# Two groups of heads, one pair of banks: where the third batch's first outputs are put

## Chip, core and metric

The kernel runs on one core of one Trainium2 chip. The metric is the device time of one execution in microseconds; lower is better. All sums of matrix products are kept in PSUM, a memory of 128 partitions with eight banks of 2 KB each; a bank holds 512 float32 per partition. TensorE (PE) writes it, VectorE (DVE) and ScalarE (ACT) read it.

## What is computed

Retention, a linear attention with a decay per head, followed by a bilinear feed-forward layer without biases:

```
q, k, v: (8 batches, 8 heads, 576 positions, 64)        float32
gamma[h] = 1 - 2**(-5-h)
scores   = (q @ k^T) / sqrt(64)
ret      = scores * gamma[h]**(i-j)   where i >= j, else 0
attn     = ret @ v
x        = attn as (8*576 = 4608 tokens, 8*64 = 512)
out      = ((x @ w_a) * (x @ w_b)) @ w_out               w_a, w_b: 512 x 1536, w_out: 1536 x 512
```

## The kernel before

**Stages.** The 4608 tokens pass through the feed-forward layer in blocks (`blocks`: 512, 256, 256, then seven of 512). `ffn_block` computes, for each of 12 slices of 128 hidden columns, a product with `w_a` (`pa`, line L794) and one with `w_b` (`pb`, L809). ACT copies the first out of PSUM (L802), and DVE multiplies it by the second (L814). Then come the products with `w_out` (`po`, L828), which ACT or DVE copy out for the store (L837, L839). Matrix operands are bfloat16, sums float32.

**Retention runs in between.** The input `x` of a block is made ahead of it by the retention of the same tokens. The first 256 positions of batches 0, 1 and 2 are done in six steps (`STEPS`): a step is one batch and one half of its heads, four heads. Steps 4 and 5 are the two halves of batch 2, and these six steps hold only the first 256 positions. Their results are the input of the second feed-forward block (tokens 512 to 767). The rest of retention runs later in larger pieces (`stretch`).

**The pieces of one step.** The positions of a step are split into an early half (`a` = 0) and a late one (`a` = 1), 128 each.

- `score_step` multiplies keys by queries within the halves (L347) into a tile `sc` of two banks. DVE masks it into `sT` (L355).
- `state_products` and `state_copies` sum keys times values into a state per half (`kv`, L374). ACT copies the first half's state to `state_after` (L386), and both states to `own` and `second` (L390, L391).
- `step_states` (L421) multiplies the late half's queries by the state after the early half: two matmuls of 128 columns that write the bank of `a` = 1.
- `step_keys` (L437) multiplies values by masked scores: 16 small matmuls (64 x 64, 128 columns), eight into each bank, added to what `step_states` left in the bank of `a` = 1.
- `close_step` (L448) scales the outputs with `qs_o` on DVE and writes them to the tile `x` of the block.

**Where outputs stand.** An output tile is `[128, 2, 512]` float32, so two whole banks, one for each `a`. A step uses the first 256 columns of each. There are eight banks: four for the pool `ps_ffn` (one each), two for `ps_sc` (one tile) and two for `ps_o` (one tile). In the third batch, `score_step(4)` takes `ps_sc` and `score_step(5, ps_o[0], "o")` takes `ps_o`. The outputs of step 4 are then opened in `ps_sc`, and those of step 5 in `ps_o`, each in the banks of its own scores. The next writer of `ps_o` is `keyed` of the first `stretch` (L538), and the next of `ps_sc` is `matched` in the same stretch (L600).

**Accumulation.** A matmul with `start=True` marks its whole bank, on the partitions it writes, as not yet written. A later one without `start` overwrites where the mark stands and adds elsewhere.

**Order.** The order of each engine's instructions is the order in which the program issues them (`manual_schedule`). `ffn_block` yields after each matmul, and a list `todo` holds the functions with the amount of work at which they are due: `third_turn` at 124, `third_states` at 128, `third_outputs` at 136, all in the output projection of the first block. The framework sets the waits between engines from the tiles that instructions read and write. Each engine works through its queue in order, so an instruction that waits holds up all behind it on its engine.

Of the kernel before, what the change touches and what calls it, by code (L numbers as in the profile page):

```python
# [18 lines left out]
def kernel(  # L19
# [108 lines left out]
    def half(i):  # L128
        return slice(64 * i, 64 * i + 64)
# [205 lines left out]
    def queries(key, r, j, a):  # L335
        return transposed[key][r, 0].rearrange(
            "p (k j s) -> p j k s", k=2, j=2)[:, j, :, half(a)]
# [71 lines left out]
    outputs = {}  # L409

    def open_step(i, place=None):
        if place is None:
            outputs[i] = ps_o[0].tile([128, 2, 512], FP32, tag="o", name="o0")
        else:
            outputs[i] = place.tile([128, 2, 512], FP32, tag="sc", name="o0")

    def step_states(i, first):

        n, hh = STEPS[i]
        for j in (0, 1):  # L420
            nc.tensor.matmul(outputs[i][:, 1, 128 * j:128 * j + 128],  # L421
                             state_after[:, n % 2, 2 * hh + j, :],
                             queries((n, hh), slice(0, 128), j, 1),
                             start=(first and j == 0), stop=True,
                             skip_group_check=True)

    def step_keys(i, fresh):

        n, hh = STEPS[i]
        vb = natural[n, hh][1]  # L430
        sT = scored.pop((n, hh))
        seen = set()
        for j in (0, 1):
            for kp in (0, 1):
                for a, r in QUADS:
                    e0 = kp * 256 + (2 * j + r) * 64
                    nc.tensor.matmul(  # L437
                        outputs[i][half(r), a, 128 * j:128 * j + 128],
                        vb[half(a), e0:e0 + 64],
                        sT[half(a), r, j, kp],  # L440
                        start=(a in fresh and (a, r) not in seen), stop=True,
                        skip_group_check=True)
                    seen.add((a, r))

    def close_step(i):
        n, hh = STEPS[i]
        cs = slice(2 * hh, 2 * hh + 2)
        nc.vector.tensor_tensor(  # L448
            x_of(256 * n, 256)[:, cs]
            .rearrange("p j (a s) -> p a j s", a=2),  # L450
            outputs.pop(i)[:, :, 0:256]
            .rearrange("p a (j s) -> p a j s", j=2),
            qs_o[:, cs]
            .rearrange("p j (a s) -> p a j s", a=2), op=ALU.mult)
# [517 lines left out]

    def third_outputs():
        open_step(4, ps_sc)
        open_step(5)
        for i in (4, 5):
            step_states(i, True)
        for i in (4, 5):
            step_keys(i, {0})
            close_step(i)  # L980

    def third_turn():
        for i in (4, 5):
# [3 lines left out]
            (112.1, cast_step, (5, Q, "act")),  # L987
            (124, third_turn, ()), (128, third_states, ()),
            (136, third_outputs, ())]
    todo += [(60 + 10 * n, total_of, (n,)) for n in (0, 1)]  # L990
    todo += [(136, total_of, (2,))]
# [74 lines left out]
```

## Time and profile before

| | |
|---|---|
| three runs | 325.1, 326.3, 326.32 us (median 326.3) |
| profiled execution | 325.12 us |
| its span, first to last instruction | 323.4 us |
| PE busy | 317.7 us (98%) |
| DVE, ACT, POOL busy | 165.8 (51%), 131.5 (41%), 118.2 us (37%) |
| products `pa`, `pb`, `po` busy on PE | 108.8, 111.5, 97.0 us |
| scaling of a step (L448) | 0.680 to 0.692 us each, six of them |
| key products of a step (L437) | 16, 0.42 us from the first's start to the last's end |
| granted clock of TensorE | 1.00 |

Times count from the start of the span. In a line of the timeline the first number is the start, the second the duration from the first of a run of like instructions to the end of the last, then engine, line, operation, tiles written and read, shapes and count; what stands in brackets is the engine's idle time before it and what ended that. Matmuls overlap on PE: the next one starts before the last one's end. In a line of the groups, the numbers behind the bar are busy time, the mean duration in ns, and the idle time just before.

### The profile page before, as it was taken

What the parts mean: (1) busy time and instruction counts of PE and PEld (TensorE: products, weight loads), DVE (VectorE), ACT (ScalarE), POOL (GpSimd) and SP (SyncE); (2) the same over time, 40 slices, a digit from 0 to 9 for tenths busy, and PEclk for the clock granted to TensorE, in tenths of its full rate; (3) what the DMA queues carried; (4) which work ended last, traced back from release to release, by engine and by line L of the source; (5) the groups of instructions that cost most, each with busy time, mean ns of one, the idle gap of its engine ahead of it and who ended that gap; (6) DMA issues with size and microseconds to landing.
All of it is one profiled execution on the core that took longest, in us unless ns stands there. A gap on an engine that the chain in (4) does not pass through costs nothing.

```text
span 323.4 us, 8669 instructions
## 1 busy us (share of the span) xinstructions
PE 317.7 (98%) x3611; PEld 164.5 (51%) x3611; DVE 165.8 (51%) x294; ACT 131.5 (41%) x293; POOL 118.2 (37%) x158
## 2 busy tenths in 40 slices
PE   7899999999999999999999999999999999999996
PEld 3564457778444555454454545454445444444444
DVE  5734445665546754835374627561666256514311
ACT  7744853463435533533253324442433243313321
POOL 4990067574655375357075206450520000000000
PEclk9999999999999999999999999999999999999999
DMA  8999999999999999999899169935740520031013
GB/s 215 256 199 205 253 233 203 199 176 206 175 233 234 217 199 244 221 227 226 180 216 191 60 155 197 205 76 146 170 108 23 108 68 2 2 97 32 1 24 108
DMA packets 145431, 50.90 MB, mean 157 GB/s; under 512 B 126704, under 2 KB 140912, under 8 KB 145392
## 3 DMA queue, kind: packets, MB, share of 16 engines
q1 hardware_dynamic: 140112, 45.37, 68.6%
q0 software_dynamic: 4752, 4.72, 8.9%
q8 instruction: 28, 0.46, 0.6%
q10 hardware_dynamic: 528, 0.26, 0.3%
q14 instruction: 11, 0.09, 0.1%
HBM read 37.75 MB, written 9.44 MB: 146 GB/s over the span
## 4 chain that ended last, share of the span: by engine, by line
PE 94%; DMA 2%; SPq 2%; ACT 1%; DVE 1%; issue 0%; DVEq 0%
PE pb L809 29%; PE po L828 29%; PE pa L794 28%; DMA qf<-in_q_dram 2%; SPq L159 2%; PE sc L600 1%; PE o L628 1%; PE o L641 1%; PE kv L538 1%; PE pa L771 1%; ACT state_after L386 0%; PE o L437 0%; PE kv L374 0%; PE sc L347 0%; PE tp L329 0%; DVE hT L814 0%
## 5 line engine op out<-in xcount | busy, mean ns | idle before, releaser
L814 DVE TENSOR_TENSOR hT<-ha,pb 128x512 bf16<-128x512 bf16 (+1 forms) x120 | 75.9, 634 | 94.2 <-PE pb L809 86.0
L802 ACT CAST ha<-pa 128x512 bf16<-128x512 f32 (+1 forms) x120 | 64.8, 543 | 115.5 <-PE pa L794 111.2
L809 PE MATMUL pb<-xT,wb_sb 128*128 128x512 bf16 (+1 forms) x480 | 111.5, 358 | 0.1
L794 PE MATMUL pa<-xT,wa_sb 128*128 128x512 bf16 (+1 forms) x468 | 108.8, 357 | 0.0
L828 PE MATMUL po<-wo_sb,hT 128*128 128x512 bf16 (+2 forms) x456 | 97.0, 368 | 0.0
L809 PEld LDWEIGHTS <-wb_sb 128*128 128x128 bf16 x480 | 47.0, 98 | 46.5 <-issue 0.3
L794 PEld LDWEIGHTS <-wa_sb 128*128 128x128 bf16 x468 | 45.1, 98 | 44.4 <-issue 0.2
L828 PEld LDWEIGHTS <-hT 128*128 128x128 bf16 x456 | 42.8, 98 | 47.1
L484 POOL CAST qkb<-qf 64x1024 bf16<-64x1024 f32 x15 | 15.4, 1030 | 67.4 <-DMA qf<-in_q_dram 61.0
L495 POOL TENSOR_TENSOR vb<-vf,vs 128x1024 bf16<-128x1024 f32 (+1 forms) x17 | 28.8, 1699 | 13.2 <-DMA vf<-in_v_dram 8.2
L839 DVE COPY osb<-po 128x512 f32<-128x512 f32 (+2 forms) x17 | 11.1, 653 | 43.2 <-PE po L828 43.2
L837 ACT COPY osb<-po 128x512 f32<-128x512 f32 (+1 forms) x21 | 12.0, 573 | 43.3 <-PE po L828 43.3
L484 POOL CAST qkb<-kf 64x1024 bf16<-64x1024 f32 (+1 forms) x17 | 15.9, 933 | 14.5 <-DMA kf<-in_k_dram 13.9
L563 DVE TENSOR_TENSOR sums<-kv,sums 128x256 f32<-128x256 f32 x44 | 18.6, 424 | 2.8 <-PE kv L538 0.8
L609 DVE TENSOR_TENSOR sT<-sc,mask 128x512 bf16<-128x512 f32 x30 | 19.5, 681 | 0.0
L488 POOL CAST qkb<-kf 64x512 bf16<-64x512 f32 (+1 forms) x34 | 18.8, 580 | 1.0
L488 POOL CAST qkb<-qf 64x512 bf16<-64x512 f32 x30 | 17.6, 614 | 0.6
L567 ACT CAST states<-sums 64x512 bf16<-64x512 f32 x26 | 16.0, 617 | 0.3
L654 DVE TENSOR_TENSOR xT<-o,qs 128x512 bf16<-128x512 f32 x24 | 15.4, 682 | 1.5 <-PE o L641 1.5
L311 POOL CAST qkb<-kf 128x512 bf16<-128x512 f32 x5 | 3.1, 614 | 16.7 <-DMA kf<-in_k_dram 16.7
L855 PE MATMUL w<-ones 128*128 128x512 bf16 x19 | 6.8, 476 | 1.5 <-DVE idxp_f L204 1.5
L355 DVE TENSOR_TENSOR sT<-sc,mask_s 128x1024 bf16<-128x1024 f32 x6 | 7.2, 1222 | 1.3 <-PE sc L347 1.2
(88 smaller groups left out, 163.9 us busy)
## 6 DMA issues: line engine op xcount, KB each, us to landing
qf<-in_q_dram SPq DMA_DIRECT2D x32, 256.0 KB, 4.8
vf<-in_v_dram SPq DMA_DIRECT2D x32, 256.0 KB, 5.1
kf<-in_k_dram SPq DMA_DIRECT2D x31, 256.0 KB, 5.0
out_dram<-osb SPq DMA_DIRECT2D x25, 256.0 KB, 2.4
out_dram<-osb SPq DMA_DIRECT2D x21, 128.0 KB, 3.0
wo_sb<-in_moe_w_out_dram POOLq DMA_DIRECT2D x3, 512.0 KB, 16.7
qf<-in_q_dram SPq DMA_DIRECT2D x8, 128.0 KB, 3.2
kf<-in_k_dram SPq DMA_DIRECT2D x8, 128.0 KB, 3.4
```

Source lines behind the costliest of these rows:

```text
L484: nc.gpsimd.tensor_copy(qkb[0:64, w, e], t[0:64, e])
L488: nc.gpsimd.tensor_copy(to[:, :, 1 - r], fro[:, :, r])
L495: nc.gpsimd.tensor_tensor(vb[:, e].rearrange("p (h d) -> p h d", d=D), t[:, e].rearrange("p (h d) -> p h d", d=D), decay[:, at], op=ALU.mult)
L563: nc.vector.tensor_tensor(sums[:, i], own, prev, op=ALU.add)
L567: nc.scalar.copy(to(half(1 - r)), fro(half(r)))
L609: nc.vector.tensor_tensor(sT[:, on].rearrange("p c k s -> p (c k) s"), sc[:, on].rearrange("p c k s -> p (c k) s"), mask3.unsqueeze(1).to_ ...
L654: nc.vector.tensor_tensor(x_of(t0, 128).rearrange("p c (a s) -> p c a s", a=2), o[:, :, :, kp].rearrange("p a c s -> p c a s"), qs[:, :, s ...
L794: nc.tensor.matmul(pa[:, 0:n], wa_sb[:, c, fs], xT[:, c], start=(c == 0), stop=(c == NC - 1))
L802: nc.scalar.copy(ha[:, 0:n], pa[:, 0:n])
L809: nc.tensor.matmul(pb[:, 0:n], wb_sb[:, c, fs], xT[:, c], start=(c == 0), stop=(c == NC - 1))
L814: nc.vector.tensor_tensor(hT[:, F, 0:n], has[F][:, 0:n], pb[:, 0:n], op=ALU.mult)
L828: nc.tensor.matmul(po[:, 0:width], hT[:, F, u * 128:(u + 1) * 128], wo_sb[:, F, cols], start=(F == 0), stop=(F == NF - 1))
```

## The change

Only `third_outputs` is changed:

```diff
     def third_outputs():
         open_step(4, ps_sc)
-        open_step(5)
+        outputs[4], outputs[5] = (outputs[4][:, :, half] for half in
+                                  (slice(0, 256), slice(256, 512)))
         for i in (4, 5):
-            step_states(i, True)
+            step_states(i, i == 4)
         for i in (4, 5):
-            step_keys(i, {0})
+            step_keys(i, {0} if i == 4 else set())
             close_step(i)
```

The outputs of step 5 no longer have a tile of their own in `ps_o`. They use columns 256 to 511 of the two banks in `ps_sc` whose columns 0 to 255 hold the outputs of step 4. Since `start` marks a whole bank, only step 4's matmuls set it; step 5's first ones find the mark and overwrite. The order of the program stays: state products of 4 and 5, key products of 4, scaling of 4, key products of 5, scaling of 5.

## Prediction

> **What bounds the kernel now.** I read the page's first and fourth parts, then the timeline of each engine around the two output products of the third batch, then the waits of PE behind them.
>
> ```profile
> PE 317.7 (98%) x3611; PEld 164.5 (51%) x3611; DVE 165.8 (51%) x294; ACT 131.5 (41%) x293; POOL 118.2 (37%) x158
> ...
> PE 94%; DMA 2%; SPq 2%; ACT 1%; DVE 1%; issue 0%; DVEq 0%
> ```
>
> PE is busy for 98% of the span and makes up 94% of the chain that ended last. So anything that makes PE stand still in the middle of the kernel is paid at the end, unless PE would have stood still later anyway. The groups of PE instructions from 48.7 us to the end answer that. Their last column is the idle time ahead of them:
>
> ```profile
> L794 PE MATMUL pa<-xT,wa_sb 128*128 128x512 bf16 (+1 forms) x432 | 100.7, 355 | 0.0
> L809 PE MATMUL pb<-xT,wb_sb 128*128 128x512 bf16 (+1 forms) x432 | 100.6, 355 | 0.1
> L828 PE MATMUL po<-wo_sb,hT 128*128 128x512 bf16 (+2 forms) x416 | 87.9, 367 | 0.0
> ```
>
> Every PE group there has 0.0 or 0.1 us of idle. There is no later wait in which a delay of PE could be lost. The place itself, on PE (start, duration, instruction, count):
>
> ```profile
> 45.28 0.29 PE L374 MATMUL kv<-vb,qkb 64*64 64x64 bf16 x16
> 45.41 0.42 PE L347 MATMUL sc<-qkT 64*64 64x128 bf16 x16
> 45.66 0.29 PE L374 MATMUL kv<-vb,qkb 64*64 64x64 bf16 x16
> 45.89 1.90 PE L828 MATMUL po<-wo_sb,hT 128*128 128x512 bf16 x8
> ...
> 47.63 0.28 PE L421 MATMUL o<-qkT,state_after 128*128 128x128 bf16 x2
> ...
> 47.91 0.27 PE L421 MATMUL o<-qkT,state_after 128*128 128x128 bf16 x2
> 48.11 0.42 PE L437 MATMUL o<-sT,vb 64*64 64x128 bf16 x16
> ...
> 48.36 0.39 PE L437 MATMUL o<-sT,vb 64*64 64x128 bf16 x16
> 48.69 1.90 PE L828 MATMUL po<-wo_sb,hT 128*128 128x512 bf16 x8
> 50.42 0.60 PE L794 MATMUL pa<-xT,wa_sb 128*128 128x256 bf16 x4
> ```
>
> The L421 pairs at 47.63 and 47.91 are the state products of steps 4 and 5. The sixteens of L437 at 48.11 and 48.36 are their key products. DVE and ACT at the same place:
>
> ```profile
> 45.50 2.36 DVE L355 TENSOR_TENSOR sT<-sc,mask_s 128x1024 bf16<-128x1024 f32 x2
> 48.58 1.29 DVE L448 TENSOR_TENSOR xT<-o,qs_o 128x512 bf16<-128x512 f32 x2 [0.72 <-PE o L437]
> ...
> 46.04 1.09 ACT L386 CAST state_after<-kv 64x128 bf16<-64x128 f32 x4 [1.13 <-PE kv L374]
> ```
>
> Today both key products run back to back on PE, and the two scalings (L448) follow on DVE while PE is already in the output projection (L828). The first scaling starts at 48.58, in the middle of step 5's key products, and holds PE up in nothing, because it reads the banks of step 4 while PE writes those of step 5.
>
> **The change, part by part.**
>
> 1. *A wait goes.* Step 5's state products used to land in the banks that held step 5's scores, so they waited for the second masking (L355) to read them out. It ends at 45.50 + 2.36 = 47.86, and the second L421 pair starts at 47.91. Two such products last 0.28 us together at 0.22 us each, so their starts lie 0.056 us apart, and without the wait the second pair would begin at 47.63 + 2 x 0.056 = 47.74. Gain: 47.91 - 47.74 = 0.17 us. Step 5's key products need that same masking, but only after step 4's are issued, when it is long over. So the key products of step 4 move from 48.11 to 47.94, and nothing else is late in their place.
>
> 2. *A wait comes.* Both steps' outputs now share the same two banks: step 4 in columns 0 to 255 of each, step 5 in columns 256 to 511. Program order is key products of step 4, scaling of step 4 (DVE reads columns 0 to 255), key products of step 5 (PE writes columns 256 to 511). The question is whether PE must wait for the read, though the columns are disjoint. This trace has the mirror case: the products of L374 for steps 4 and 5 also share two banks, in disjoint columns. ACT copies step 4's states first. These products end at 45.57, and ACT had stood idle for 1.13 us. Yet its first copy starts at 46.04, when step 5's products in the other columns have ended too (about 45.96). So a reader here is ordered behind writes to other columns of its bank that stand ahead of it in the program. I take it that a writer is ordered behind such a reader in the same way.
>
> 3. *Its price.* From the first L437 of step 4 to the start of its scaling it takes 48.58 - 48.11 = 0.47 us. The scaling takes 0.69 us (L448: six of 0.680 to 0.692). The handover from DVE to PE is 0.05 us, by the masking that ends at 47.86 and the product that starts at 47.91. So step 5's key products start at 47.94 + 0.47 + 0.69 + 0.05 = 49.15, where today they start at 48.36. That is **0.79 us late**, with the gain of part 1 already in it. In-order behind the waiting instruction stand the eight L828 and, after them, the second block's first products (L794): 48.69 becomes 49.48, and 50.42 becomes 51.21. Bounds: without the wait, -0.17 us. Upwards, if the 64x64 weight loads (0.1 us each) can't be done ahead of the wait either, one of them is added: +0.9 us.
>
> 4. *What else moves.* No instruction is added or taken away on any engine, no DMA is issued, and the two `start` flags that go change no duration. Step 5's scaling can start 0.44 us after its first key product (48.36 to about 48.80 today, by the end of the products), so at 49.59, and ends at 50.28. Today it ends at 48.58 + 1.29 = 49.87. It must be there before L794 reads its result: today with 0.55 us to spare, afterwards with 51.21 - 50.28 = 0.93 us. So no second wait grows from it. Behind the scaling, on DVE, are a sum (L405, 0.42 us) and a copy of an output (L839). Both have time, since the copy's product on PE is 0.79 us later as well. The freed banks get their next writer at 56.7 us (L538), and PE isn't idle ahead of it, so freeing them early brings nothing. The shared banks are next written at 57 us (L600), long after 50.28. POOL, ACT and the DMA queues wait for PE at most 0.79 us longer, and what they deliver is wanted by PE 0.79 us later.
>
> **Sum.** The profiled execution took 325.12 us (span 323.4 us, 1.7 us around it). It becomes 325.12 + 0.79 = 325.9 us. The three runs read 325.1, 326.3 and 326.32, and the profiled one lies at the low end of them. I add the 0.79 us to their median: **327.1 us**, 0.24% more. That is less than the 0.5% that a measurement of this kernel can tell from no change.
>
> **Two rules weighed.** On part 2, the row is ACT's start at 46.04. It could have another reading, that only PE's signal came late and not that banks are kept apart. The Trainium skill, page "PSUM — Partial Sum Buffer", section "PSUM bank collisions raise a hardware error", says that two engines on the same bank and quadrant collide even at disjoint columns, and that the compiler back end orders such pairs. That speaks against this change: by the rule the sum is +0.79 us, by the other reading -0.17 us. On the clock, the longest standstill of PE that the trace shows once it runs fast is under 0.5 us from start to start (ahead of L347 at 14.15, and no slow stretch follows). The new one is from about 48.2 to 49.15, so nearly 1 us. The page "TensorE: Matmul & The Clock Gate", table "The two states you'll see", halves the clock only after an idle window of about 3.4 us. By it nothing is added, and no row here has a standstill of that length in mid-kernel.
>
> **The rivals.**
>
> *The standstill slows PE's clock (slower).* The trace shows a slow PE at the start, after 1.52 us of idleness:
>
> ```profile
> 1.52 3.40 PE L855 MATMUL w<-ones 128*128 128x512 bf16 x8 [1.52 <-DVE idxp_f L204]
> 4.90 0.40 PE L329 MATMUL tp<-identity,qkb 128*128 128x128 bf16 x4
> ```
>
> Eight matmuls of 512 columns take from 1.52 to 4.90, so 3.38 us. Later the chain has 28 of that form (L828) in 6.04 us, 0.216 each, so eight would take 1.73 us. One such slow stretch costs 3.38 - 1.73 = 1.65 us. With the wait that makes 0.79 + 1.65 = 2.44 us: 328.7 us, 0.75% slower. It decides if a standstill of nearly 1 us is enough; for it speaks that only 1.5 us of idleness stands ahead of the slow start, against it that PE's standstills of up to 0.5 us left no trace and that the new one is shorter than 1.5 us. The granted clock would not tell, since it reads 1.00 in the first 4 us too; the distance between starts would.
>
> *No new wait (the change does what its layout suggests).* If order is kept by columns and not by banks, only part 1 remains: 326.3 - 0.17 = 326.1 us. For it speaks that the columns are disjoint, against it the copy at 46.04.
>
> *The delay is lost on the way.* The only later standstills of PE worth naming stand at 78 to 80 us, by the distances between starts about 0.6 us in all, ahead of L794 and L809, while they wait for ACT and DVE. These wait for PE in their turn and would come late with it, so little can be lost there. If all of it were: 326.3 + 0.79 - 0.6 = 326.5 us.
>
> **How the numbers follow.** The wait of 0.79 us: 0.66. The slowed clock: 0.18. No wait: 0.08. Lost on the way: 0.04. A gain that I see no row for: 0.04. The runs of before scatter over 1.2 us, so of the 0.66 I put 0.08 above the bound of 0.5% (1.6 us). Slower: 0.18 + 0.08 = 0.26. Same: 0.58 + 0.08 + 0.04 = 0.70. Faster: 0.04. The range goes from a little below the wait on top of the lowest run (325.1 + 0.79 = 325.9, and 0.3 below for the cases under it) to the slowed clock: 325.6 to 328.8 us.
>
> **What would show it.** In the changed kernel's timeline: four L421 without a gap, sixteen L437 at about 47.94, one L448, a hole in PE of about 0.95 us, sixteen L437 at about 49.15, then L828 at 49.48. L448 would come apart into two single rows a good microsecond from start to start. After 49.48 every row of PE should lie 0.79 us later than before. I am wrong if the sixteens of L437 still stand back to back, if the starts of L828 behind them lie 0.43 us apart and not 0.216, or if a hole shows further on that isn't there now.

## The result, and the profile after

The changed kernel takes **326.34 us** (median of 15 runs, 326.06 to 327.72), the kernel before 325.37 us (median of 15, 325.1 to 326.48). The ratio is 1.003 with a 95% interval of 1.0019 to 1.0041: a small loss of 0.6 to 1.3 us, less than 0.5%. Forecast was no change within 0.5%, with 0.79 us more.

The profiled execution took 326.23 us, its span is 324.5 us, 1.1 us longer than before. The page's first and fourth parts:

```profile
PE 314.4 (97%) x3573; PEld 165.0 (51%) x3611; DVE 165.4 (51%) x294; ACT 131.5 (41%) x293; POOL 118.3 (36%) x158
...
PE 95%; issue 1%; ACT 1%; DVE 1%; DVEq 0%
```

PE still makes up nearly the whole chain. That it counts 3573 matmuls and not 3611 is no change of the program: 38 records are missing from this trace (the weight loads are all there), so its busy time and its small "issue" holes are not to be compared. The starts are.

The timeline of PE at the changed place:

```profile
45.68 0.42 PE L347 MATMUL sc<-qkT 64*64 64x128 bf16 x16
...
47.89 0.39 PE L421 MATMUL o<-qkT,state_after 128*128 128x128 bf16 x4
48.20 0.42 PE L437 MATMUL o<-sT,vb 64*64 64x128 bf16 x16
49.42 0.42 PE L437 MATMUL o<-sT,vb 64*64 64x128 bf16 x16 [0.80 <-DVE xT L448]
49.77 1.90 PE L828 MATMUL po<-wo_sb,hT 128*128 128x512 bf16 x7
51.51 0.60 PE L794 MATMUL pa<-xT,wa_sb 128*128 128x256 bf16 x4
```

and of DVE:

```profile
48.68 0.69 DVE L448 TENSOR_TENSOR xT<-o,qs_o 128x512 bf16<-128x512 f32 x1 [0.56 <-PE o L437]
49.88 0.69 DVE L448 TENSOR_TENSOR xT<-o,qs_o 128x512 bf16<-128x512 f32 x1 [0.52 <-PE o L437]
```

The four state products (L421) now follow one another. The key products of the two steps have come apart: the second sixteen start at 49.42, after an idle time of 0.80 us that a DVE scaling ended. That scaling runs from 48.68 to 49.37. The two scalings have come apart in the same way.

**Where the 1.1 us of the span come from.** Step 5's score products (L347) started at 45.41 before and start at 45.68 now, so 0.27 us of the difference are there already before the changed place. Up to about 43 us all kernels of this study issue the same program, and yet the start of that group differs by up to 0.9 us from one profiled execution to the next (45.41 to 46.32), and by 2.2 us in split, where a stretch of slow clock at 16 us adds to it (see there). before_twice, whose outputs stand as in the kernel before, starts the group at 46.14, and after_twice, which has the change, at 45.45. So this part goes with the execution, not with the change. From that group to the first L794 it took 50.42 - 45.41 = 5.01 us before and takes 51.51 - 45.68 = 5.83 us now: **0.82 us** are lost at the changed place. At the end of the span it is 0.83 us by the same measure (1.1 - 0.27), so nothing was won back or lost on the way.

This distance, from the start of step 5's score products to the start of the first `pa` product of the second block, serves for all kernels below. It is read from the starts of PE's matmuls:

| kernel | score products of step 5 | first `pa` of block 2 | beside the kernel before |
|---|---|---|---|
| before | 45.41 | 50.42 | 0 |
| changed | 45.68 | 51.51 | +0.82 |
| keys_first | 46.32 | 51.16 | -0.17 |
| filled | 45.89 | 50.96 | +0.06 |
| split | 47.62 | 53.51 | +0.88 |
| after_twice | 45.45 | 52.01 | +1.55 |
| before_twice | 46.14 | 51.15 | 0.00 |
| by_bank | 45.46 | 51.94 | +1.47 |
| two_tiles | 45.48 | 51.19 | +0.70 |
| after_three | 45.57 | 54.41 | +3.83 |
| after_four | 45.90 | 55.07 | +4.16 |
| after_six | 45.70 | 57.03 | +6.32 |

### The profile page after: what moved, and what is told of

It is laid out like the page before. It is cut to its first block, busy times and chain, and to the rows that moved or that the text cites. A ratio compares the mean times of both kernels' runs of the same rounds, so it can differ in the third digit from the quotient of the medians.

```text
span 324.5 us, 8631 instructions
## 1 busy us (share of the span) xinstructions
PE 314.4 (97%) x3573; PEld 165.0 (51%) x3611; DVE 165.4 (51%) x294; ACT 131.5 (41%) x293; POOL 118.3 (36%) x158
## 4 chain that ended last, share of the span: by engine, by line
PE 95%; issue 1%; ACT 1%; DVE 1%; DVEq 0%
PE pb L809 29%; PE po L828 29%; PE pa L794 28%; PE sc L600 1%; PE o L628 1%; PE w L855 1%; PE o L641 1%; PE kv L538 1%; PE tp L329 1%; PE pa L771 1%; PE o L437 1%; PE sc L347 1%; PE kv L374 0%; ACT qkT L333 0%; ACT state_after L386 0%
## 5 line engine op out<-in xcount | busy, mean ns | idle before, releaser
L794 PE MATMUL pa<-xT,wa_sb 128*128 128x512 bf16 (+1 forms) x452 | 106.9, 356 | 1.2 <-issue 0.6
L828 PE MATMUL po<-wo_sb,hT 128*128 128x512 bf16 (+2 forms) x442 | 94.7, 367 | 1.7 <-issue 1.4
L794 PEld LDWEIGHTS <-wa_sb 128*128 128x128 bf16 x468 | 45.1, 98 | 44.4 <-issue 0.2
L828 PEld LDWEIGHTS <-hT 128*128 128x128 bf16 x456 | 42.7, 98 | 47.2
L609 DVE TENSOR_TENSOR sT<-sc,mask 128x512 bf16<-128x512 f32 x30 | 19.4, 681 | 0.0
```

The lines of the kernel that those rows point to most:

```text
L609: nc.vector.tensor_tensor(sT[:, on].rearrange("p c k s -> p (c k) s"), sc[:, on].rearrange("p c k s -> p (c k) s"), mask3.unsqueeze(1).to_ ...
L794: nc.tensor.matmul(pa[:, 0:n], wa_sb[:, c, fs], xT[:, c], start=(c == 0), stop=(c == NC - 1))
L828: nc.tensor.matmul(po[:, 0:width], hT[:, F, u * 128:(u + 1) * 128], wo_sb[:, F, cols], start=(F == 0), stop=(F == NF - 1))
```

## Experiments

The theory: PE stands until DVE has read step 4's columns, because the program puts that read ahead of step 5's key products and both steps use the same banks. Rival A: sharing the banks costs by itself, whatever the order. Rival B: the 0.27 us at the start belong to the change. Rival C: the standstill slows PE's clock. In kernels with an added helper the line numbers behind it are 5 to 18 higher (L828 is then L833 or L836, and the half scaling is L459).

### keys_first: both key products ahead of both scalings

```diff
         for i in (4, 5):
             step_keys(i, {0} if i == 4 else set())
+        for i in (4, 5):
             close_step(i)
```

> The layout of the changed kernel (both steps in one pair of banks), but with both steps' key products ahead of both scalings. Theory: the cost is PE standing behind DVE's read of step 4's columns, so with no read between the two key products there is no standstill. The four L421 follow one another, the thirty-two L437 follow one another, and PE is 0.17 us ahead of the kernel before from there on: 325.2 us beside 325.4, ratio 0.9995. The first scaling now waits for step 5's products too, and starts about 0.2 us later than in the kernel before relative to PE; both end some 0.3 us before L794 needs them. Rival A: sharing the banks costs by itself, whatever the order: ratio 1.003 stays. Rival B: a part of the loss, the 0.26 us that the changed kernel's trace is late by already at 16 us, belongs to the change: ratio about 1.0003.

Measured: 325.39 us beside 325.25, ratio 0.9995 (0.9986 to 1.0005). PE:

```profile
48.85 0.64 PE L437 MATMUL o<-sT,vb 64*64 64x128 bf16 x32
49.42 1.90 PE L828 MATMUL po<-wo_sb,hT 128*128 128x512 bf16 x8
51.16 0.60 PE L794 MATMUL pa<-xT,wa_sb 128*128 128x256 bf16 x4
```

All thirty-two key products are one group, with L828 right behind. The place is 0.17 us shorter than in the kernel before, to the hundredth what part 1 of the prediction gave for the removed wait. The banks are shared as in the changed kernel, so sharing costs nothing by itself: rival A falls. Rival B expected a ratio of 1.0003, which lies within the interval, so the timed runs don't decide it. The table does: the start of that group is late by 0.04 us in after_twice, by 0.73 us in before_twice, which has no change, and by 0.91 us here, so the delay there doesn't go with the change.

### filled: four output products between the two key products

```diff
         for i in (4, 5):
             step_states(i, i == 4)
-        for i in (4, 5):
-            step_keys(i, {0} if i == 4 else set())
-            close_step(i)
+        step_keys(4, {0})
+        close_step(4)
+    def third_rest():
+        step_keys(5, set())
+        close_step(5)
...
-            (136, third_outputs, ())]
+            (136, third_outputs, ()), (137, third_rest, ())]
```

> The changed kernel, but step 5's key products and scaling are issued four L828 (0.86 us) later than step 4's scaling. Theory: the scaling runs beside those four L828, the wait has only about 0.05 us left, and two more changes between kinds of matmul cost 0.1 us each; 0 to 0.2 us more than the kernel before, ratio 1.000 to 1.0006. The scaling of step 5 then ends only just before L794 reads it (under 0.1 us to spare). Rival A (sharing costs by itself): ratio 1.003.

Measured: 325.56 us beside 325.25, ratio 1.0005 (0.9996 to 1.0014).

```profile
48.42 0.42 PE L437 MATMUL o<-sT,vb 64*64 64x128 bf16 x16
48.77 1.04 PE L828 MATMUL po<-wo_sb,hT 128*128 128x512 bf16 x4
49.73 0.42 PE L437 MATMUL o<-sT,vb 64*64 64x128 bf16 x16
```

No hole is left: the second sixteen follow the four L828, and the scaling has run beside these. The place costs 0.06 us: from the first L437 to L794 it takes 2.54 us here and 2.31 us in keys_first, so the two more changes between kinds of matmul cost 0.23 us, and 0.17 us of that are won back at L421. The order of the program still has the read ahead of the write, but the read has ended (48.89 + 0.69 = 49.58, by the timeline of DVE) before PE comes to the second sixteen at 49.73.

### split: step 4's scaling in two halves, one for each bank

```diff
-            close_step(i)
+        for part in (0, 1):
+            close_half(4, part)      # outputs[4][:, part, 0:256] only
+        step_keys(5, set())
+        close_step(5)
```

> The changed kernel with step 4's scaling as two DVE instructions of 128x256, one for each bank. If PE is ordered by the bank, the first L437 of step 5, which writes the first bank, starts after the first half scaling (about 0.4 us after the scaling began), and the second L437, which writes the second bank, stands until the other half has ended. If it is ordered by the tile as a whole, all sixteen start after the second half. In both cases the standstill in sum is that of the changed kernel plus at most 0.1 us: span 324.5 to 324.6 us, less whatever the first 16 us differ by.

```profile
50.62 0.75 DVE L459 TENSOR_TENSOR xT<-o,qs_o 128x256 bf16<-128x256 f32 x2 [0.56 <-PE o L437]
51.43 0.42 PE L437 MATMUL o<-sT,vb 64*64 64x128 bf16 x16 [0.86 <-DVE xT L459]
```

All sixteen start after the second half (50.62 + 0.75 = 51.37). That points to a wait for the whole tile, but DVE signals only once in this trace, after the second half, so it is not settled by this run. The place costs 0.88 us, 0.06 us more than in the changed kernel, like the scaling (0.75 against 0.69). Its one execution took 328.37 us (span 326.7), which says nothing more, since 2.2 us of that were lost before 45 us. Most of these went into a stretch of slow clock long before the changed place. The last idle time of PE ahead of it, and the stretch itself, with the granted clock as the number ahead of the last two:

```profile
15.34 1.03 PE L374 MATMUL kv<-vb,qkb 64*64 64x64 bf16 x16 [0.49 <-ACT vb L319]
...
16.00:19.00 3.00, 2.95 (x50) 2.10 (x49) 1.39 (x3) 1.71 (x9) 3.00 (x5) 0.50 1.01 137
```

The granted clock reads 0.50 from 16.0 to 19.4 us, and 3.4 us at half pace lose 1.7 us. In the other profiles it reads 1.00 there.

### after_twice and before_twice: the price doubled, with its control

Both issue step 4's scaling twice, in the changed kernel and in the kernel before:

```diff
+            for again in range(1 if i == 4 else 0):
+                scaled_again(i)      # close_step(i), and outputs[i] stays
             close_step(i)
```

> The changed kernel with step 4's scaling issued twice (the same result, written twice). Two such scalings in a row take 1.29 us in the kernel before, so the second adds 0.61 us. Theory: all of it stands on PE's path: the hole in PE grows from 0.80 to about 1.41 us, and the time is 0.97 + 0.61 = 1.58 us over the kernel before, ratio 1.0048. Rival A (sharing costs by itself): ratio 1.003 stays. Rival C (a longer standstill slows the clock): the L828 behind the hole start 0.43 us apart and the ratio goes to 1.009.

> The kernel before with step 4's scaling issued twice, the control to the changed kernel with the same doubling. Theory: with banks of its own for each step no matmul waits for the first scaling, so the added 0.6 to 0.7 us lie beside L828; step 5's scaling has 0.55 us to spare ahead of L794, so 0 to 0.2 us are seen: ratio 1.000 to 1.0006. Rival: if the doubled scaling costs its length by itself (DVE is short of time here), ratio 1.002.

Measured: 326.91 us beside 325.25, ratio 1.0051 (1.0031 to 1.0071), for the changed kernel with the doubling; 325.58 beside 325.54, ratio 1.0002 (0.9993 to 1.0012), for the control. The hole in the first of them:

```profile
47.98 0.42 PE L437 MATMUL o<-sT,vb 64*64 64x128 bf16 x16
49.92 0.42 PE L437 MATMUL o<-sT,vb 64*64 64x128 bf16 x16 [1.52 <-DVE xT L448]
```

and the control, DVE and PE:

```profile
49.31 2.01 DVE L448 TENSOR_TENSOR xT<-o,qs_o 128x512 bf16<-128x512 f32 x3 [0.72 <-PE o L437]
...
48.84 0.64 PE L437 MATMUL o<-sT,vb 64*64 64x128 bf16 x32
```

The hole grew from 0.80 to 1.52 us, by 0.72 and not by the 0.61 expected: the second scaling, which writes the same result again, starts only when the first has ended (1.42 us for two, where the kernel before has 1.29 for two that read and write different places). The place grew by 1.55 - 0.82 = 0.73 us. In the control the same instruction costs 0.00 us at the place. So it is the position on PE's path that makes the scaling dear, not DVE's time.

The control shows one thing more. Its step 5 scaling ends at 51.32 (49.31 + 2.01), and yet the first `pa` product of the second block starts at 51.15. The first two of that slice's four matmuls read the half of `xT` that step 4's scaling writes; the third, which reads step 5's half, starts at 51.38. So on `xT` a matmul did not wait for a scaling that writes another part of the same tile.

### by_bank and two_tiles: what the wait is bound to

by_bank keeps the shared banks and the two-bank tile, and orders the work by bank (`step_keys` is given the banks that it shall write):

```diff
         step_keys(4, {0})
+        close_half(4, 1)
+        step_keys(5, set(), (0,))
+        close_half(4, 0)
+        step_keys(5, set(), (1,))
         close_step(5)
```

> The shared banks again, with this order: key products of step 4; DVE scales step 4's second bank (a = 1); step 5's eight key products into the first bank (a = 0); DVE scales step 4's first bank; step 5's eight key products into the second bank; scaling of step 5. The run with the scaling in halves could not tell a wait by bank from a wait by tile, since DVE signalled only once, after both halves. If PE is ordered by the bank, the first eight follow step 4's without a wait, and only the last eight stand until the scaling of the second bank is over, about 0.93 us after step 4's first L437: L828 comes about 0.4 us later than in the kernel before, ratio 1.0013. If it is ordered by the tile of two banks, there are two holes, one of some 0.5 us ahead of the first eight and one of some 0.7 us ahead of the last eight, and L828 is about 1.3 us late, ratio 1.004.

Measured: 326.96 us beside 325.54, ratio 1.0047 (1.0032 to 1.0062).

```profile
47.99 0.42 PE L437 MATMUL o<-sT,vb 64*64 64x128 bf16 x16
48.94 0.41 PE L437 MATMUL o<-sT,vb 64*64 64x128 bf16 x8 [0.53 <-DVE xT L459]
49.86 0.41 PE L437 MATMUL o<-sT,vb 64*64 64x128 bf16 x8 [0.51 <-DVE xT L459]
```

Two holes. The first eight write the first bank, and the only read that stands ahead of them is one of the second bank. They wait for it all the same, and here each half scaling has a wait of PE of its own behind it, so it is no matter of one signal for both.

two_tiles has the same order and the same sharing, but each bank is a tile of its own:

```diff
-        open_step(4, ps_sc)
-        outputs[4], outputs[5] = (outputs[4][:, :, half] for half in
-                                  (slice(0, 256), slice(256, 512)))
+        banks = [ps_ffn.tile([128, 512], FP32, tag="ab", name=f"o4{a}")
+                 for a in (0, 1)]
+        outputs[4], outputs[5] = InTwo(banks, 0), InTwo(banks, 256)
```

> The order of the run by_bank (scaling of the second bank, step 5's eight key products into the first bank, scaling of the first bank, eight into the second), but the two banks are two tiles of one bank each, taken from the pool of the feed-forward products. Both steps still share each bank. In by_bank PE waited ahead of the first eight though no read of their bank stood before them. If the order is kept by the tile, the first eight now follow step 4's key products without a wait, and one hole of about 0.5 us stands ahead of the last eight, until the scaling of the second bank is over. If something else made the first eight wait (DVE's signal, or the fact that both steps share the banks), the two holes of 0.5 us stay. The time itself tells little here, since two of the four banks of the feed-forward products are lent for a while and the first L421 may wait up to 0.4 us for a bank.

```profile
48.16 0.64 PE L447 MATMUL o<-sT,vb 64*64 64x128 bf16 x24
49.11 0.41 PE L447 MATMUL o<-sT,vb 64*64 64x128 bf16 x8 [0.31 <-DVE xT L469]
```

Sixteen and eight run as one group of 24, and one hole is left, ahead of the last eight. So the wait on these outputs is bound to the tile: in by_bank a read of one bank of the two-bank tile held back a write to the other. Within a tile of one bank, the last eight of two_tiles still wait, though they write other columns than the read takes. Both readings come from one profiled execution each, and two_tiles also scales step 5 in halves and takes its tiles from another pool. (The place costs 0.70 us there; the first L421 also waited for its lent bank, as expected. The single execution took 325.91 us, beside one of 325.35 for the kernel before. A layout with one bank for each step wasn't tried.)

### after_three, after_four, after_six: how long a standstill slows the clock

The doubling of after_twice, with three, four and six scalings.

> The changed kernel with step 4's scaling issued three times: a hole of 0.80 + 2 x 0.72 = 2.25 us. The hole of 1.52 us left the clock alone, the one of 2.97 us was followed by about 3.4 us at half the pace. Paid by its length alone: everything behind is 0.83 + 1.44 = 2.3 us later than in the kernel before, relative to the state at 48 us, and L828 start 0.216 us apart. With the slow stretch: 1.7 us more and starts 0.43 us apart.

> The changed kernel with step 4's scaling issued four times. Doubling added 0.72 us to the hole in PE, so three more give a hole of 0.80 + 3 x 0.72 = 2.96 us. If the hole were paid only by its length: everything behind is 0.83 + 2.16 = 3.0 us later than in the kernel before, less whatever the first 16 us differ by, and the L828 behind it start 0.216 us apart. If a hole of 3 us slows the clock: the starts are 0.43 us apart for a stretch, and up to 1.65 us come on top.

> The changed kernel with step 4's scaling issued six times, so a hole of 0.80 + 5 x 0.72 = 4.4 us in PE. The same question with a longer standstill. Paid by its length alone: 0.97 + 3.6 = 4.6 us over the kernel before, ratio 1.014, starts of L828 0.216 us apart. With a slowed clock behind it: 0.43 us apart for about 3.4 us, up to 1.65 us more, ratio 1.019.

Measured: after_six 332.08 us beside 325.54, ratio 1.0195 (1.0173 to 1.0217). after_three and after_four have one execution each, of 329.39 us (span 327.7) and 330.68 us (span 329.0). The hole of after_three and what follows it:

```profile
50.76 0.42 PE L437 MATMUL o<-sT,vb 64*64 64x128 bf16 x16 [2.25 <-DVE xT L448]
51.11 3.50 PE L833 MATMUL po<-wo_sb,hT 128*128 128x512 bf16 x8
54.41 0.73 PE L799 MATMUL pa<-xT,wa_sb 128*128 128x256 bf16 x4
```

Eight L833 take from 51.11 to 54.41, so 3.30 us, where eight take 1.73 us elsewhere: from the second on, their starts lie 0.43 us apart. The granted clock of after_four from 52 to 56 us, the number ahead of the last two:

```profile
52.00:56.00 4.00, 3.78 (x28) 1.83 (x21) 2.34 (x3) 0.40 (x1) 3.96 (x4) 0.59 1.05 175
```

By the granted clock in stretches of 1 us, taken as either full or half, the slow time is 3.4 us for a hole of 2.25 us, 3.4 us for 2.97 us, and 6.8 us for 4.42 us. In the first two it begins when PE has been at work again for 0.5 us (from 51.24 us on) and 0.9 us (from 52.72 us on), in the third within the hole. After 1.52 us (after_twice) and 0.80 us (changed kernel) the clock reads 1.00, and the starts of L833 and L828 lie 0.216 us apart. The loss fits: measured at the first L538, some 6 us further on, where the slow time of after_three and after_four is over, they are 3.96 and 4.68 us late. The holes by their length explain 0.82 + 2 x 0.72 = 2.26 and 0.82 + 3 x 0.72 = 2.98. What is left is 1.70 us both times, half of 3.4.

So rival C describes a real effect. But the length of one standstill doesn't set its limit. In split a slow stretch of the same 3.4 us stands at 16 us, with no standstill of PE above 0.49 us in the 8 us ahead of it, while after_twice had 1.52 us without one. And of the four executions of after_six, all with the same program, two have a mean granted clock of 0.99 (332.64 and 332.28 us) and two of 0.994 and 0.995 (331.22 and 331.88 us). One slow stretch of 3.4 us goes with 0.995 in after_three and after_four, so the latter two probably had one and the former two had two. What decides it stays open. The changed kernel shows none: its granted clock is 0.999 or 1.00 in all 15 executions.

## Why the prediction was right, and where it was not

**Part 1, the wait that goes: right.** 0.17 us forecast, -0.17 us in keys_first. In the changed kernel, the key products of step 4 start at 48.20, with the 0.27 us of the start taken off at 47.93; forecast 47.94.

**Part 2, the wait that comes: it came, but not bound to what I said.** I read from ACT's late copy at 46.04 that order is kept by the bank. The tiles in that row are of one bank each, so the row could not tell bank from tile. by_bank and two_tiles tell: it is the tile. For this change both give the same wait. Whoever had used the reading to plan a way out by working bank by bank within the tile would have got by_bank, 0.47% slower than before.

**Part 3, its price: right.** 0.79 us forecast, 0.82 us measured at the place. From key products to scaling 0.48 us (0.47), the scaling 0.69, the handover 0.05. The 0.03 us more are spent behind the hole: from the sixteen to the next L828 it takes 0.35 us where the unbroken row has 0.33, and the rest is rounding.

**Part 4, nothing else late: right.** The second scaling starts at 49.88 (49.61 without the start; forecast 49.59), L794 at 51.51 (51.24; forecast 51.21), and the distance stays the same to the end of the span. before_twice shows the spare time on DVE that this rests on. That time was even longer than I said: I counted to the first L794, but only the third one reads what step 5's scaling writes.

**The sum: the size right, the base too high.** I added the 0.79 us to the median of three runs, 326.3. Of all 15 runs, these three among them, the median is 325.37, so two of my three were high ones and the profiled execution, 325.12, was the usual one. Based on that, the sum would have been 325.9; the measured 326.34 lies between the two. The timed loss of 0.97 us and the 0.82 us of the trace agree within the interval (0.6 to 1.3).

**The rivals.** The slowed clock had 0.18 and didn't occur in any of the 15 executions. after_three shows it after a standstill of 2.25 us and split after none above 0.49 us, so the shortness of the 0.80 us alone, which I held against this rival, doesn't exclude it. For its price I had 1.65 us from the first matmuls, and the experiments gave 1.70. The rule I quoted from the Trainium skill, page "TensorE: Matmul & The Clock Gate", table "The two states you'll see", was right about this change, but its idle window of about 3.4 us is too long as a limit here: a standstill of 2.25 us was enough in after_three. No new wait (0.08), and a delay lost on the way (0.04): neither is in the trace.

**What the change could have had.** The same layout with the key products ahead of the scalings (keys_first) has no standstill. It frees a pair of banks from the end of the second masking to the next L538 at no cost that the runs show, at 0.9995 (0.9986 to 1.0005) of the kernel before; a gain is not shown.

## What to carry to other kernels

Where two results share a tile in PSUM, put all writes ahead of all reads in the program, or put other work of the writer between a read and the next write; disjoint columns, and even disjoint banks of one tile, bought no freedom here. When PE is busy throughout, the price of such a wait is read off beforehand from three rows: last write to start of the read, the read, and the handover back. To tell one execution's own delay from the change's, measure the distance between two events on either side of the changed place, and not the span.

## What the runs showed of the hardware

In these kernels one standstill of PE of 2.25 us and one of 2.97 us were each followed by 3.4 us at half pace, beginning 0.5 and 0.9 us after PE had resumed; one of 4.42 us went with twice that time, and one of 1.52 us left no trace. Each of these was profiled in one execution, and no limit follows from them: split had 3.4 us at half pace at 16 us after standstills of at most 0.49 us, and after_six seems to have had one slow stretch in two of its executions and two in the other two. In these stretches the granted clock shows it (0.59 over four microseconds in after_four), while the first matmuls of the kernel, equally 0.43 us apart, run under a reading of 1.00. And a profiled execution was late by up to 0.9 us at 45 us although the program up to there is the same, without any slow stretch; why stays open.
